# Normalising an attention group one step later in a software pipeline

## The chip, the cores and the metric

The kernel runs on one core of a Trainium2 chip. The metric is the device time of one execution in microseconds (us); lower is better. A core has TensorE (PE, matrix products and transposes), VectorE (DVE), ScalarE (ACT), GpSimd (POOL) and SyncE (SP, which issues the transfers here). Each engine works through its own list of instructions in order, and they wait for each other through semaphores.

## The reference

Sliding-window attention with a few sink tokens, then two gated layers:

```python
scores = scale * q @ k.T                      # 2 x 8 heads, 768 tokens, head size 64
keep = is_sink | in_window                    # 4 sinks, window of 128
a = exp(where(keep, scores, -1e9) - rowmax)
a = a / (sum(a) + 1e-9)
x = (a @ v)  -> [1536, 512]
x = (silu(x @ w_gate) * (x @ w_val)) @ w_out            # 512 -> 1536 -> 512
h = x @ w_in; out = (max(h,0) + alpha * min(h,0)) @ w_out2   # 512 -> 2048 -> 512
```

The inputs are normal random numbers; weights come as 64-bit floats and are split on the chip into a high and a low half for three matrix products in place of one.

## The kernel before

Attention is cut into 24 groups: one batch, one pair of heads, two blocks of 128 queries each (`NG` = 2). Eight groups of the first kind (query blocks 0 and 1) have no separate sinks and come first; from group 8 on a group has sink columns of its own. `attention` is a software pipeline of 27 steps. In step x it issues, in this order:

- `scores(x)`: four score products on PE (L217, tile `ps_s`); on DVE for each its masked row maximum (L223, for the later kind after a masked copy L221); on ACT its exponentials with row sums (L227, tiles `pr` and `ssum`);
- `values(x-3)`: the products of probabilities and values on PE (L313, L316, tile `xp`), then ACT's copy `xh` (L805) and DVE's remainder `xl` (L806);
- `flips(x-2)`: transposes of the normalised probabilities on PE (L272, and L295 for the sinks), copied out of PSUM into `pt`: groups 0 to 7 by ACT (L280) and DVE (L278), later ones by ACT (L283, L296) and then cut at the window by two selects on POOL (L284, L288);
- `norm(x)`: on DVE the row sums plus epsilon (L243) and their inverse (L244, tile `rinv`), and on POOL the products of `pr` with it (L250 for groups 0 to 7, L259 and the sinks' L260 for later ones). PE's flips of the group need these products.

Between these places the caller (`fast`) puts the work of the weight stream and of the first layer. One weight tile costs ACT a scaled copy (L520), DVE three bit operations (L536, L539, L542), ACT the high half (L550) and POOL the low half `wl` (L557). Such a conversion stands behind the flips in steps 2, 4, 6 and 7. From step 10 on the first layer's products (L613 to L615, L681 to L683) are mixed in, so PE has other work beside the attention; after the last group PE goes through the two layers alone.

DVE's list keeps the order in which the program is written (a manual schedule). The lists of PE, ACT, POOL and SP are set by a scheduler that works with its own model of times. PSUM has eight buffers (`ps`), shared by all: a product that finds none free waits for the reader of an old one. `pr` and `sk` have three buffers, `ssum` and `rinv` four, `pt` two.

Of the kernel before, what the change touches and what calls it, by code (L numbers as in the profile page):

```python
# [321 lines left out]
def attention(groups, begin):  # L322
    n = len(groups)

    def stage(f, x):
        if x < n:
            return getattr(groups[x], f)()

    stage("load", 0)
    begin[0]()  # L330
    stage("load_v", 0)
    stage("load", 1)
    stage("load", 2)
    begin[1]()
    for x in range(n + LAG + 1):
        if x < n:
            for t in range(NG):
                groups[x].scores(t)
        yield "before values", x, x - LAG - 1
        if x > LAG:  # L340
            groups[x - LAG - 1].values()
        yield "values", x, x - LAG - 1
        if LAG <= x < n + LAG:
            for t in range(NG):
                groups[x - LAG].flip(t)
        yield "flips", x, x - LAG - 1
        if x < n:
            groups[x].norm()
        stage("load", x + 3)
        stage("load_v", x + 1)  # L350
        if x == 14:
            begin[2]()
# [422 lines left out]
def fast(nc, tc, ctx, g, lim, alpha, qk, vp, vs, w_gate, w_val, w_out, x2_in, x2_out, out):  # L775
# [21 lines left out]
    with ExitStack() as inner:  # L797
# [26 lines left out]
        for at, x, last in attention(groups, (begin_a, begin_b, begin_c)):  # L824
            done = max(0, last + (at != "before values"))
            if at == "values" and done in (per, 2 * per):
                ready.append(m1.unit(0, done // per - 1))
            if done < per:
                if at == "flips" and st.n_conv < EARLY:
                    st.tick(1 + (done > 1))  # L830
            elif at == "before values" or at == "flips" and x in TWICE:
                product()
# [105 lines left out]
```

## Time and profile before

| | us |
|---|---|
| median of 3 runs | 683.36 (682.8 to 683.9) |
| the profiled execution, its own time | 680.56 |
| its span, first to last instruction | 678.8 |
| PE busy in the span | 657.4 (97%) |
| DVE busy | 391.7 (58%) |
| ACT busy | 297.8 (44%) |
| POOL busy | 79.9 (12%) |
| mean granted TensorE clock | 0.987 of full speed |

How to read it: every duration below is of this one profiled execution, whose own time is 680.56 us; 1.8 us of it lie outside the span. PE is close to full over the whole, but matmuls are pipelined, and the mean says little of the first stage, in which PE is free for about a fifth of the time. What any edit of the attention is worth has to be read there and in the mixed stage behind it.

### The profile page before, as it was taken

What the parts mean: (1) busy time and instruction counts of PE and PEld (TensorE: products, weight loads), DVE (VectorE), ACT (ScalarE), POOL (GpSimd) and SP (SyncE); (2) the same over time, 40 slices, a digit from 0 to 9 for tenths busy, and PEclk for the clock granted to TensorE, in tenths of its full rate; (3) what the DMA queues carried; (4) which work ended last, traced back from release to release, by engine and by line L of the source; (5) the groups of instructions that cost most, each with busy time, mean ns of one, the idle gap of its engine ahead of it and who ended that gap; (6) DMA issues with size and microseconds to landing.
All of it is one profiled execution on the core that took longest, in us unless ns stands there. A gap on an engine that the chain in (4) does not pass through costs nothing.

```text
span 678.8 us, 8589 instructions
## 1 busy us (share of the span) xinstructions
PE 657.4 (97%) x3098; PEld 519.5 (77%) x3098; DVE 391.7 (58%) x880; ACT 297.8 (44%) x680; POOL 79.9 (12%) x137
## 2 busy tenths in 40 slices
PE   7889889999999999999999999999999999999996
PEld 4555666767788888888888888888888888888885
DVE  5896858444289932389432789419834744334332
ACT  4778765656366612155221546336622333112320
POOL 3554644333100000000000000000000000000000
PEclk8989899999999999999999999999999999999998
DMA  9653535200045520045200034203400000000111
GB/s 264 180 169 115 166 114 168 69 24 24 1 155 186 169 79 1 0 125 181 68 0 1 33 124 129 89 1 93 156 1 0 1 0 1 1 0 8 55 63 67
DMA packets 37203, 52.29 MB, mean 77 GB/s; under 512 B 4384, under 2 KB 28960, under 8 KB 37152
## 3 DMA queue, kind: packets, MB, share of 16 engines
q1 hardware_dynamic: 34944, 51.65, 24.0%
q8 instruction: 26, 0.43, 0.2%
q10 hardware_dynamic: 2208, 0.01, 0.2%
q14 instruction: 25, 0.20, 0.1%
HBM read 48.51 MB, written 3.15 MB: 76 GB/s over the span
## 4 chain that ended last, share of the span: by engine, by line
PE 84%; DVE 7%; ACT 5%; issue 1%; POOL 1%; DMA 1%; SPq 0%; ACTq 0%; POOLq 0%
PE ph L615 6%; PE ph L613 6%; PE pf L739 6%; PE pf L737 6%; PE pf L738 6%; PE ph L614 6%; PE po L681 5%; PE po L682 5%; PE po L683 5%; PE pv L613 4%; PE pg L613 4%; PE pv L615 4%; PE pv L614 4%; PE pg L614 4%; PE pg L615 4%; PE xp L313 2%
## 5 line engine op out<-in xcount | busy, mean ns | idle before, releaser
L626 ACT ACTIVATE hh<-hid 128x512 fp32r<-128x512 f32 x84 | 53.1, 632 | 70.5 <-DVE hid L665 41.2
L627 DVE TENSOR_TENSOR hl<-hid,hh 128x512 fp32r<-128x512 f32 x84 | 57.9, 689 | 36.5 <-ACT hh L626 36.4
L613 PE MATMUL ph<-yh,wh 128*128 128x512 f32 x192 | 74.8, 390 | 0.0
L615 PE MATMUL ph<-yh,wl 128*128 128x512 f32 x192 | 74.7, 389 | 0.0
L737 PE MATMUL pf<-wh,hh 128*128 128x512 f32 x192 | 74.7, 389 | 0.0
L738 PE MATMUL pf<-wl,hh 128*128 128x512 f32 x192 | 74.7, 389 | 0.0
L614 PE MATMUL ph<-yl,wh 128*128 128x512 f32 x192 | 74.7, 389 | 0.0
L719 ACT ACTIVATE neg<-ph,sal 128x512 f32<-128x512 f32 x48 | 33.0, 687 | 93.4 <-PE ph L615 93.4
L739 PE MATMUL pf<-wh,hl 128*128 128x512 f32 x192 | 72.1, 389 | 0.0
L550 ACT ACTIVATE wh<-w_m 128x512 fp32r<-128x512 f32 x68 | 42.6, 630 | 55.8 <-DVE w_m L542 17.4
L721 DVE SCALAR_TENSOR_TENSOR hid<-ph,sig,neg 128x512 f32<-128x512 f32 x48 | 35.9, 749 | 38.4 <-ACT neg L719 38.0
L613 PE MATMUL pg<-xh,wh 128*128 128x512 f32 x144 | 57.6, 401 | 0.0
L613 PE MATMUL pv<-xh,wh 128*128 128x512 f32 x144 | 56.9, 395 | 0.3 <-ACT pt L283 0.3
L614 PE MATMUL pg<-xl,wh 128*128 128x512 f32 x144 | 57.0, 396 | 0.0
L615 PE MATMUL pg<-xh,wl 128*128 128x512 f32 x144 | 56.6, 393 | 0.0
L681 PE MATMUL po<-hh,wh 128*128 128x512 f32 x144 | 56.5, 394 | 0.0
L614 PE MATMUL pv<-xl,wh 128*128 128x512 f32 x144 | 56.2, 391 | 0.0
L682 PE MATMUL po<-hh,wl 128*128 128x512 f32 x144 | 56.2, 391 | 0.0
L615 PE MATMUL pv<-xh,wl 128*128 128x512 f32 x144 | 56.1, 390 | 0.0
L744 DVE TENSOR_TENSOR acc<-pf,acc 128x512 f32<-128x512 f32 x36 | 23.2, 686 | 52.0 <-PE pf L739 52.0
L683 PE MATMUL po<-hl,wh 128*128 128x512 f32 x144 | 53.2, 390 | 0.0
L557 DVE TENSOR_TENSOR wl<-w_m,wh 128x512 fp32r<-128x512 f32 x56 | 38.2, 686 | 21.6 <-ACT wh L550 21.5
(106 smaller groups left out, 1198.0 us busy)
## 6 DMA issues: line engine op xcount, KB each, us to landing
w_raw<-in_moe_w_out SPq DMA_DIRECT2D x28, 512.0 KB, 3.4
w_raw<-in_moe_w_in SPq DMA_DIRECT2D x16, 512.0 KB, 3.8
w_raw<-in_moe_w_gate SPq DMA_DIRECT2D x12, 512.0 KB, 3.7
w_raw<-in_moe_w_val SPq DMA_DIRECT2D x12, 512.0 KB, 3.6
th<-in_qk SPq DMA_DIRECT2D x16, 336.0 KB, 3.0
vr<-in_v SPq DMA_DIRECT2D x16, 192.0 KB, 2.4
out<-acc SPq DMA_DIRECT2D x12, 256.0 KB, 2.2
th<-in_qk SPq DMA_DIRECT2D x8, 256.0 KB, 5.5
```

Of the source, the lines that this page charges most:

```text
L550: nc.scalar.activation(wh, m, AF.Copy)
L613: nc.tensor.matmul(ps, wh[:, c], xh[:, kk], start=(kk == 0), stop=False)
L614: nc.tensor.matmul(ps, wh[:, c], xl[:, kk], start=False, stop=False)
L615: nc.tensor.matmul(ps, wl[:, c], xh[:, kk], start=False, stop=(kk == KD - 1))
L626: nc.scalar.activation(hh, hid, AF.Copy)
L627: nc.vector.tensor_tensor(out=hl, in0=hid, in1=hh, op=ALU.subtract)
L681: nc.tensor.matmul(ps, wh[:, mc], hh, start=(x == 0), stop=False)
L682: nc.tensor.matmul(ps, wl[:, mc], hh, start=False, stop=False)
L683: nc.tensor.matmul(ps, wh[:, mc], hl, start=False, stop=(x == CHUNK - 1))
L737: nc.tensor.matmul(ps, hh[:, ts], wh, start=(x == 0), stop=False)
L738: nc.tensor.matmul(ps, hh[:, ts], wl, start=False, stop=False)
L739: nc.tensor.matmul(ps, hl[:, ts], wh, start=False, stop=(x == CHUNK - 1))
```

## The change

`norm` is issued for group x-1 instead of group x, in the same place of step x, and so there is one more of its places at the end (step 24) and none in step 0:

```diff
         yield "flips", x, x - LAG - 1
-        if x < n:
-            groups[x].norm()
+        if 0 < x <= n:
+            groups[x - 1].norm()
         stage("load", x + 3)
```

The first place is DVE's list in step 3 (names end in a running number; `ps_s` is a score tile, `ssum` the row sums that the exponentials leave, `rinv` the inverse). Before, from the first maximum of group 3 on:

```order
L223 ISA ps_s_271,nb_111<-ps_s_271,mask_0_68 128x128
L223 ISA ps_s_272,nb_111<-ps_s_272,mask_0_68 128x128
L223 ISA ps_s_279,nb_111<-ps_s_279,mask_1_69 128x256
L223 ISA ps_s_280,nb_111<-ps_s_280,mask_1_69 128x256
L806 TENSOR_TENSOR xl_91<-xp_287,xh_90 128x256
L278 COPY pt_294<-ps_p_299 128x2x256
L243 TENSOR_SCALAR rinv_308<-ssum_269 128x4
L244 RECIPROCAL rinv_308<-rinv_308 128x4
```

After, the same stretch:

```order
L223 ISA ps_s_266,nb_111<-ps_s_266,mask_0_68 128x128
L223 ISA ps_s_267,nb_111<-ps_s_267,mask_0_68 128x128
L223 ISA ps_s_274,nb_111<-ps_s_274,mask_1_69 128x256
L223 ISA ps_s_275,nb_111<-ps_s_275,mask_1_69 128x256
L806 TENSOR_TENSOR xl_91<-xp_282,xh_90 128x256
L278 COPY pt_289<-ps_p_294 128x2x256
L243 TENSOR_SCALAR rinv_303<-ssum_218 128x4
L244 RECIPROCAL rinv_303<-rinv_303 128x4
```

The kinds of instruction stand in the same order; only the last two work on other data. Before, `ssum_269` belongs to group 3, whose maxima stand just above; after, `ssum_218` belongs to group 2, and the inverse of group 3 comes one step later.

The second place is POOL's list around steps 14 and 15 (`pt_1195` before and `pt_1189` after are the transposed probabilities of group 13, `pr_1010` and `pr_1004` the probabilities of group 14). Before:

```order
L288 AFFINE_SELECT pt_1070<-pt_1070 128x2x128
L259 TENSOR_TENSOR pr_1010<-pr_1010,rinv_1115 128x2x2x128
L260 TENSOR_TENSOR sk_1118<-pr_1010,rinv_1115 128x128
L557 TENSOR_TENSOR wl_1109<-w_m_1055,wh_1108 128x512
L284 AFFINE_SELECT pt_1195<-pt_1195 128x2x128
```

After:

```order
L557 TENSOR_TENSOR wl_1103<-w_m_1049,wh_1102 128x512
L284 AFFINE_SELECT pt_1189<-pt_1189 128x2x128 x2
L288 AFFINE_SELECT pt_1189<-pt_1189 128x2x128 x2
L259 TENSOR_TENSOR pr_1004<-pr_1004,rinv_1206 128x2x2x128
L260 TENSOR_TENSOR sk_1209<-pr_1004,rinv_1206 128x128
```

The normalising products of group 14 stood ahead of the selects of group 13 and now stand behind them.

The third place is PE's list in step 16, where group 13's values end and group 14 is transposed. Before:

```order
L316 MATMUL xp_1261<-pts_1208,vsr_113 128x128 x2
L272 MATMUL ps_p_1273<-ident_61,pr_1010 128x128 x2
L272 MATMUL ps_p_1279<-ident_61,pr_1010 128x128 x2
L681 MATMUL po_1246<-hh_944,wh_1177 128x512
L295 MATMUL ps_p2_1286<-ident_61,sk_1118 128x128
L681 MATMUL po_1289<-hh_679,wh_963 128x512
```

After:

```order
L316 MATMUL xp_1255<-pts_1202,vsr_113 128x128 x2
L681 MATMUL po_1240<-hh_938,wh_1171 128x512
L272 MATMUL ps_p_1267<-ident_61,pr_1004 128x128 x2
L272 MATMUL ps_p_1273<-ident_61,pr_1004 128x128 x2
L295 MATMUL ps_p2_1280<-ident_61,sk_1209 128x128
L681 MATMUL po_1283<-hh_673,wh_957 128x512
```

One product of the first layer (L681) has moved ahead of the transposes. PE's list up to step 13 is the same as before.

## Rows read from the trace of the kernel before

**Rows 1.** Stretches: length, busy us of PE, PEld, DVE, ACT, POOL, then PEclk, DMA.
```profile
0.00:48.50 48.50, 39.66 (x213) 23.92 (x214) 38.36 (x158) 30.55 (x116) 23.50 (x37) 0.89 0.69 204
48.50:110.00 61.50, 56.03 (x301) 38.44 (x299) 44.28 (x142) 43.49 (x121) 31.01 (x48) 0.97 0.46 145
110.00:180.00 70.00, 68.95 (x409) 49.88 (x406) 30.18 (x120) 38.90 (x113) 25.40 (x53) 1.00 0.15 45
180.00:678.80 498.80, 492.70 (x2183) 407.22 (x2181) 278.91 (x465) 184.86 (x331) 0.00 (x0) 1.00 0.19 61
```

**Rows 2.** Waits: who waited for whom, us in total, times, longest us.
```profile
DVE rinv L243 <- ACT pr L227: 4.1, 5, 1.7
```

**Rows 3.** Timeline, DVE, first inverse: start, duration, form, [idle before and releaser].
```profile
10.40 0.17 DVE L243 TENSOR_SCALAR rinv<-ssum 128x4 f32<-128x4 f32 x1 [1.67 <-ACT pr L227]
```

**Rows 4.** Timeline, PE, transposes of groups 0, 3, 5 and 8.
```profile
12.60 0.86 PE L272 MATMUL ps_p<-ident,pr 128*128 128x128 f32 x4 [0.52 <-POOL pr L250]
...
24.33 0.88 PE L272 MATMUL ps_p<-ident,pr 128*128 128x128 f32 x6
...
33.24 1.43 PE L272 MATMUL ps_p<-ident,pr 128*128 128x128 f32 x6
...
48.05 0.66 PE L272 MATMUL ps_p<-ident,pr 128*128 128x128 f32 x4
```

**Rows 5.** Timeline, DVE, steps 6 to 9: copies of flips, one bit operation, inverses.
```profile
31.65 0.68 DVE L278 COPY pt<-ps_p 128x512 f32<-128x512 f32 x1
32.25 0.42 DVE L536 TENSOR_SCALAR w_m<-w_m 128x512 int32<-128x512 int32 x1
...
34.04 0.16 DVE L243 TENSOR_SCALAR rinv<-ssum 128x4 f32<-128x4 f32 x1
...
35.87 0.68 DVE L278 COPY pt<-ps_p 128x512 f32<-128x512 f32 x1
36.47 1.24 DVE L536 TENSOR_SCALAR w_m<-w_m 128x512 int32<-128x512 int32 x1
...
42.11 0.68 DVE L278 COPY pt<-ps_p 128x512 f32<-128x512 f32 x1
...
45.74 0.68 DVE L278 COPY pt<-ps_p 128x512 f32<-128x512 f32 x1
```

**Rows 6.** Timeline, POOL, step 6: normalising products, then a weight's low half.
```profile
34.58 1.61 POOL L250 TENSOR_TENSOR pr<-pr,rinv 128x256 f32<-128x256 f32 x2 [4.05 <-DVE rinv L244]
36.15 1.27 POOL L557 TENSOR_TENSOR wl<-w_m,wh 128x512 fp32r<-128x512 f32 x1
```

**Rows 7.** Stretch of 2 us, columns as in Rows 1.
```profile
34.00:36.00 2.00, 2.00 (x10) 1.53 (x10) 1.97 (x13) 2.00 (x9) 1.42 (x2) 0.50 0.53 119
```

**Rows 8.** Timeline, POOL, normalising products of groups 12, 14 and 15.
```profile
75.08 1.04 POOL L259 TENSOR_TENSOR pr<-pr,rinv 128x512 f32<-128x512 f32 x1 [2.91 <-DVE rinv L244]
...
96.23 1.04 POOL L259 TENSOR_TENSOR pr<-pr,rinv 128x512 f32<-128x512 f32 x1 [3.91 <-DVE sig L98]
...
106.01 1.04 POOL L259 TENSOR_TENSOR pr<-pr,rinv 128x512 f32<-128x512 f32 x1 [4.90 <-ACT wh L550]
```

**Rows 9.** Timeline, PE, transposes of groups 11, 13 and 14.
```profile
76.34 0.60 PE L272 MATMUL ps_p<-ident,pr 128*128 128x128 f32 x4
...
96.52 0.60 PE L272 MATMUL ps_p<-ident,pr 128*128 128x128 f32 x4
98.82 0.33 PE L295 MATMUL ps_p<-ident,sk 128*128 128x128 f32 x1 [1.70 <-ACT pr L227]
...
104.76 0.38 PE L272 MATMUL ps_p<-ident,pr 128*128 128x128 f32 x2
105.60 0.44 PE L272 MATMUL ps_p<-ident,pr 128*128 128x128 f32 x2 [0.46 <-DVE xl L806]
```

**Rows 10.** Timeline, DVE, two later inverses: groups 13 and 15.
```profile
81.16 0.37 DVE L243 TENSOR_SCALAR rinv<-ssum 128x4 f32<-128x4 f32 x1 [1.04 <-ACT pr L227]
...
105.46 0.16 DVE L243 TENSOR_SCALAR rinv<-ssum 128x4 f32<-128x4 f32 x1
```

## The prediction

> **What bounds the kernel now.** I read the busy times by stretch first. From 180 us on (498.8 us) PE works on the two layers alone, at full clock, busy for 492.7 us; no attention is left there, and nothing in it changes. From 110 to 180 us PE is busy for 68.95 of 70 us. Only ahead of that does PE have time to spare: 8.8 us of the first 48.5, in which it has nothing but attention and DVE is the fuller engine beside it (38.4 busy), and 5.5 us of the next 61.5, the mixed stage [rows 1]. So the change can matter by what it does to the length of the first stage, and by stalls of PE in the mixed one; from there on a delay of PE goes to the end almost whole, since 1.05 us of idle time is all that could take it up before 180 us.
>
> Next the waits. DVE's sum (L243) waits for ACT's exponentials five times, 4.1 us in all [rows 2]; this is what the edit can take away. The first of them is the largest: at 10.40 us DVE has stood for 1.67 us while the scores of group 1 were already there [rows 3]. What the edit gives in exchange is distance: before, the normalising products of a group are issued two steps ahead of its transposes, after, one. So the other question for the trace is how long PE's transposes stand behind POOL's products, and I went through the first stage and the mixed one transposition by transposition.
>
> **The change part by part.** No instruction is added or removed, 24 pairs L243/L244 and POOL's products stay. The SP list has its loads in nearly the old order, and loads are not what these steps wait for; I cost that at nothing.
>
> *First stage, the gain.* DVE goes from the maxima of group 0 straight to those of group 1, 1.67 us plus the two instructions earlier, about 2.0. The inverse of group 0 is still taken at about 10.4, because ACT's sums come then, so its transposes are unchanged at 12.60 to 13.46 [rows 3, 4].
>
> *First stage, the price: a new loop.* From there step follows step by one chain: DVE copies the transposes of group x-2, then takes the inverse of group x-1, POOL multiplies, PE transposes that group, DVE copies it in the next step. Its links: copy to next DVE instruction 0.60 (31.65 to 32.25); start of L243 to start of POOL 0.54 (34.04 to 34.58); POOL 1.61 [rows 5, 6]; the last four of six transposes, 0.88 x 4/6 = 0.59 at full clock [rows 4]; two hand-overs, 0.15 together (POOL ends at 12.55, PE goes on at 12.60, and as much again to DVE, an estimate from that). Sum 3.5 us. In a step with a weight's bit operations 1.79 comes on top (32.25 to 34.04): 5.3 us.
>
> Now the copies one after the other. Group 0: 13.55 (transposes end at 13.46). Step 2 has bit operations: group 1 at 18.85; group 2 at 22.35; step 4: 27.65; 31.15; step 6: 36.45. Step 7 to step 8 DVE's own work is longer than the loop: before it takes 6.24 (35.87 to 42.11), of which 0.82 is L536 at 1.24 in place of 0.42, so 5.4: group 6 at 41.9; and 3.63 (42.11 to 45.74) for group 7: 45.5. Before, this last copy is at 45.74 [rows 5]. The inverse of group 8 follows at 46.1, POOL's 1.04 (length as in [rows 8]) ends at about 47.7, and group 8's transposes can start then; before they start at 48.05 [rows 4]. The early 2.0 us are used up by the loop, and by this sum the stage ends 0.35 early. My links are short estimates at two places, so I take 0. Bounds: -2.0 (the loop is hidden and the early gain stays) and +1.4 (0.2 more on each of the seven loops).
>
> One place where the Trainium skill bears on this. L536 took 1.24 us where it takes 0.42 otherwise, and ended 0.3 after POOL's L557 of 1.27, which had begun 0.32 us ahead of it [rows 5, 6]. The Trainium skill, page "SBUF — State Buffer", section "Who interferes with whom", says that VectorE in its two-port modes and GpSimd take their shared pair of ports in turn, each for a whole instruction; by that rule the trace agrees. By it the loop would lose up to about 1.1 us more (1.27 less 0.16) wherever a low half falls on the inverse, and the sum would be +3.1 with one such meeting; without one, as I have it, +2.0.
>
> *First stage, PE's clock.* The loop now holds PE's transposes, and PE stands before them for longer at a time (it waits for POOL with the scores and values done). In this trace PE's granted clock falls to half, 1.2 GHz, after such thinly filled times: it is 0.50 from 34 to 36 us, and six transposes take 1.43 instead of 0.88 [rows 4, 7]. Before, DVE and not PE bounds those steps, so it is hidden. In the loop one such stretch costs at least 0.37 (four of six transposes), and up to 1.5 if the scores behind them, also at half speed, push the next transposes back. One or two more or less costly stretches: +0.6, bounds 0 and +3.
>
> *Mixed stage.* PE has products of the first layer between the attention's, so most transposes find their probabilities ready: I compare each start on PE with the place on POOL where, after, that group's products will stand (those of the next group now). Group 11: POOL ends at 76.12, PE starts at 76.34, 0.2 to spare. Group 13: POOL would end at 97.27, PE starts at 96.52, late by 0.75; but PE stands until 98.82 for PSUM behind these transposes, so it costs nothing. Group 14: POOL begins at 106.01 and ends at 107.05, because DVE reaches that inverse at 105.46 only, behind two weight conversions; PE is there at 104.76 [rows 8 to 10]. After, both pairs run from 107.1 to 107.7 where before they end at 106.04, 1.66 later; less 0.23 for the one product now ahead of them (492.7 us for 2183 recorded matmuls [rows 1]): +1.4 us of PE. Bounds: 0 (DVE comes there earlier) and 107.1 - 104.76 = 2.3. For the other groups 0, bounds 0 and +1.4 (a second one like group 14).
>
> *Mixed stage, the gain.* The largest wait here, 1.04 at 81.16 [rows 10], lets, once gone, the maxima of group 14 begin 1 us earlier, but ACT, which has to follow, is itself held by its list. I take 0, bound -2.4 (all 4.1 but the first 1.67).
>
> Sum: 0 + 0.6 + 1.4 + 0 = +2.0 us on the profiled execution's 680.56, 682.6. That execution lies 2.8 below the median of the runs; the same +2.0 on 683.36 gives 685.4.
>
> **The rivals.**
>
> *Level.* PE's stall at group 14 is taken up later (group 13's 0.75 already costs nothing, and 1.05 us of idle time lies at 110 to 180), and the clock does no worse than before: 683.4, within 0.6. For it: the first stage comes out level link by link, and a stall of the in-order PE hits only one group of 24. Against: DVE's place for that inverse is set by its list, and nothing in the change moves it forward.
>
> *Faster.* The removed waits are worth more than the distance: the 2.0 us of the first step stay, because the loop is shorter than I add up (its hand-overs, or POOL's first product letting the first transposes go). Its price is decided in steps 2 to 5: if the copy of group 3 comes 2 us ahead of its 27.65, the gain stays. Time 683.36 - 2.0 = 681.4. For it: 4.1 us of waits do go, and no work is added. Against: the loop, whose links are each a row.
>
> *The clock falls more often.* PE waits longest in the steps with bit operations, of which the loop has four; two or three of them end in a stretch at half clock, each with 1 to 1.5 us on the loop: +3 in the first stage, and 1.4: 683.36 + 4.4 = 687.8. For it: the mean clock is 0.89 in the thinly filled first stage and 1.00 from 110 us on, where PE is full [rows 1]. Against: it falls after some thin times only, and PE's work per step is the same as before. The Trainium skill, page "TensorE: Matmul & The Clock Gate", section "What's actually happening", says that the low clock is the default and that activity releases it; the rows agree in their direction, and by that rule this case would be the likelier one.
>
> **How the numbers follow.** A difference below 0.2% (1.4 us) can't be told from no change here. The forecast, slower by about 2 (from 0.8 to 3.3): 0.50. Level: 0.26. Faster: 0.11. The clock: 0.13. Of the forecast's share about a fifth lies under 1.4 us: slower 0.50 x 0.8 + 0.13 + 0.02 (from the top of level) = 0.55; the same 0.10 + 0.24 = 0.34; faster 0.11. Likeliest: 685.4, its own range 684.1 to 686.7. The range reaches down to 682.3 (half of the faster case left out) and up to 688.2 (the clock case in).
>
> **What would show it.** Right: no wait of L243 for the exponentials; the maxima of group 1 at about 8.7 us (10.40 less 1.67); in steps 3 to 7 PE's transposes and DVE's copies waiting for POOL's L250; the transposes of group 8 at 48 to 49 us; those of group 14 waiting for POOL until DVE has passed two weight conversions, 1 to 2 us. Wrong: group 8's transposes earlier than 47 or later than 50 us, or group 14's without a wait; or a different length after 180 us, where I count no change.

## The result, and the profile after

| | before | after |
|---|---|---|
| median of 6 runs each, us | 682.87 (680.47 to 683.9) | 686.83 (685.26 to 688.09) |
| the profiled execution, own time | 680.56 | 688.09 |
| its span | 678.8 | 686.3 |
| mean granted TensorE clock | 0.987 | 0.979 |

The ratio of the runs is 1.0066 [1.0042, 1.0089]: slower by 4.5 us (2.9 to 6.1) on 682.87 us, where +2.0 was forecast. The two medians are 4.0 us apart. (Below, a ratio is turned into us in the same way.) Executions far off the rest of their kernel (704.5 and 2704.5 us of the changed kernel with zero products, 823.3 us of the mixed half, 1649.5 us of the kernel before) are in none of the ratios; the profiled execution of after is the slowest of its six, and that of before lies within 0.1 us of its fastest. Between these two the difference is 7.5 us, and what the two traces show has to be read with that in mind.

The stretches of after, columns as in [rows 1] (length, busy us of PE, PEld, DVE, ACT, POOL, then PEclk and DMA):

```profile
0.00:48.50 48.50, 37.67 (x195) 21.18 (x197) 33.95 (x142) 28.91 (x109) 20.70 (x33) 0.79 0.66 196
48.50:110.00 61.50, 53.41 (x295) 36.47 (x293) 44.38 (x137) 41.77 (x115) 28.83 (x43) 0.97 0.43 132
110.00:180.00 70.00, 68.30 (x387) 49.02 (x388) 34.14 (x136) 39.47 (x121) 28.28 (x55) 0.98 0.21 62
180.00:686.30 506.30, 500.05 (x2225) 412.79 (x2223) 279.38 (x466) 187.14 (x337) 2.42 (x7) 1.00 0.19 60
```

In the first 48.5 us every engine gets less done than in [rows 1], and the granted clock is 0.79 instead of 0.89. From 180 us on the program is only shifted.

The waits of after, up to 190 us (who waited for whom, us in total, times, longest), with the sum's own wait from the view of DVE as the last row:

```profile
PE ps_p L272 <- POOL pr L250: 7.8, 10, 1.9
DVE pt L278 <- PE ps_p L272: 6.4, 6, 1.7
PE ps_p L272 <- POOL pr L259: 2.5, 3, 1.3
...
DVE rinv L243 <- ACT pr L227: 0.4, 1, 0.4
```

The 4.1 us of [rows 2] have become 0.4. In their place PE's transposes wait for POOL's products and DVE's copies for the transposes: the loop that the prediction described. DVE's list around the first inverse (start, duration, form, idle before and releaser), answering to [rows 3]:

```profile
8.60 0.32 DVE L223 CUSTOM_DVE_ANT_0 ps_s<-ps_s,mask 128x128 f32<-128x128 f32 x1
...
10.38 0.17 DVE L243 TENSOR_SCALAR rinv<-ssum 128x4 f32<-128x4 f32 x1 [0.39 <-ACT pr L227]
```

The maxima of group 1 begin at 8.60 (8.7 was forecast), the inverse is taken at the old time. PE's transposes of groups 3 to 8 (the first row of each), as in [rows 4]:

```profile
26.19 0.60 PE L272 MATMUL ps_p<-ident,pr 128*128 128x128 f32 x2 [1.94 <-POOL pr L250]
...
31.30 1.54 PE L272 MATMUL ps_p<-ident,pr 128*128 128x128 f32 x6
...
36.48 0.64 PE L272 MATMUL ps_p<-ident,pr 128*128 128x128 f32 x2 [1.81 <-POOL pr L250]
...
42.24 0.69 PE L272 MATMUL ps_p<-ident,pr 128*128 128x128 f32 x2
...
47.43 0.88 PE L272 MATMUL ps_p<-ident,pr 128*128 128x128 f32 x6
...
51.67 0.66 PE L272 MATMUL ps_p<-ident,pr 128*128 128x128 f32 x4 [0.58 <-POOL pr L259]
```

Group 8 starts 3.6 us later than in [rows 4]; 48 to 49 us was forecast, and "later than 50" was named as the sign of an error. The clock of the stretches between (columns as above, PEclk third from the end):

```profile
26.00:28.00 2.00, 1.41 (x6) 0.93 (x6) 0.89 (x5) 1.78 (x9) 2.00 (x3) 0.58 0.85 244
28.00:30.00 2.00, 2.00 (x12) 1.12 (x12) 1.52 (x8) 1.16 (x5) 0.87 (x2) 0.50 0.14 48
...
34.00:36.00 2.00, 0.67 (x8) 0.29 (x4) 1.93 (x7) 1.00 (x3) 0.18 (x1) 1.00 0.51 136
...
40.00:42.00 2.00, 2.00 (x12) 0.77 (x8) 1.90 (x8) 0.63 (x1) 0.43 (x1) 0.50 0.07 13
...
44.00:46.00 2.00, 2.00 (x10) 1.19 (x8) 1.42 (x6) 1.20 (x6) 0.88 (x2) 0.50 0.61 218
```

In both places PE has just waited (1.94 and 1.81 us), and then its clock goes to half (1.2 GHz): from about 26 to 33 us and again from about 37 to 47. Before, the like of it are two shorter spells, of about 3 us each, around 34 to 36 [rows 7] and 44 to 46. The change also moved some of ScalarE's copies in this stage; whether that costs anything is answered below, by a run that has them nearly in the same places.

PE in the mixed stage, groups 13 and 14, answering to [rows 9], and a stretch behind:

```profile
101.43 0.66 PE L272 MATMUL ps_p<-ident,pr 128*128 128x128 f32 x4 [1.33 <-POOL pr L259]
103.32 0.30 PE L295 MATMUL ps_p<-ident,sk 128*128 128x128 f32 x1 [1.23 <-ACT pr L227]
...
110.06 0.49 PE L681 MATMUL po<-hh,wh 128*128 128x512 f32 x1 [1.06 <-ACT wh L550]
...
111.15 0.66 PE L272 MATMUL ps_p<-ident,pr 128*128 128x128 f32 x4 [0.59 <-POOL pr L259]
```
```profile
112.00:114.00 2.00, 2.00 (x6) 1.59 (x6) 1.33 (x7) 1.85 (x9) 2.00 (x5) 0.50 0.78 263
```

Group 13's L295 stands 4.5 us later than in [rows 9], group 14's L295 (111.64, before 106.26) 5.4, and group 15's first transpose (123.29, before 115.60) 7.7; from there to the end the shift stays at 7.5 to 7.7. So in this execution the first stage lost 3.6 us and the mixed stage 4.1. Of the latter, 2.3 us are lost between groups 14 and 15, with the clock at half from 112 to 115 us, where it was at 1.00 before; 0.9 up to group 13, most of it between groups 11 and 12, where both kernels have a spell at half clock of the same length; and 0.9 between groups 13 and 14.

### The profile page after: what moved, and what is told of

Read it like the earlier page. It is cut to its first block, busy times and chain, and to the rows that moved or that the text cites. A ratio compares the mean times of both kernels' runs of the same rounds, so it can differ in the third digit from the quotient of the medians.

```text
span 686.3 us, 8590 instructions
## 1 busy us (share of the span) xinstructions
PE 659.4 (96%) x3098; PEld 519.5 (76%) x3098; DVE 391.9 (57%) x880; ACT 297.3 (43%) x680; POOL 80.2 (12%) x137
## 4 chain that ended last, share of the span: by engine, by line
PE 85%; DVE 4%; ACT 4%; POOL 3%; issue 1%; DMA 1%; SPq 0%; POOLq 0%; ACTq 0%
PE ph L613 6%; PE ph L615 6%; PE pf L739 6%; PE pf L737 6%; PE pf L738 6%; PE ph L614 6%; PE po L681 5%; PE po L682 5%; PE po L683 5%; PE pv L613 4%; PE pg L613 4%; PE pv L614 4%; PE pv L615 4%; PE pg L614 4%; PE pg L615 4%; PE ps_s L217 2%
## 5 line engine op out<-in xcount | busy, mean ns | idle before, releaser
L681 PE MATMUL po<-hh,wh 128*128 128x512 f32 x144 | 57.4, 401 | 1.1 <-ACT wh L550 1.1
```

What stands on the lines that cost most here:

```text
L681: nc.tensor.matmul(ps, wh[:, mc], hh, start=(x == 0), stop=False)
```

## The experiments

Each kernel ran beside the kernel before on the same chip. What they have in common first: where PE's granted clock was below 1.00 from 20 to 50 us in the profiled execution, when group 8's transposes started in it, and the time of all runs against before.

| kernel | clock below 1.00 | group 8, us | against before, us |
|---|---|---|---|
| before | 32 to 38, 42 to 48 | 48.05 | |
| after | 26 to 34, 36 to 48 | 51.67 | +4.5 |
| first stage only | 26 to 34, 36 to 48 | 51.36 | +3.9 |
| after, group 14 in its old step | 26 to 32, 36 to 42 | 49.70 | +4.5 |
| before with zero products | none | 47.97 | -0.1 |
| first stage only with zero products | none | 47.70 | -1.8 |
| normalised ahead of the values | 36 to 48 | 47.89 | -3.7 |
| the same with zero products | none | 47.82 | -3.3 |

### Which half of the change costs it

Groups 0 to 7 alone one step later:

```diff
-        if x < n:
-            groups[x].norm()
+        for y in ([x - 1] if 0 < x < 9 else [8, 9] if x == 9 else [x] if 9 < x < n else []):
+            groups[y].norm()
```

> The inverse comes one step later for groups 0 to 7 only (the first stage); in step 9 groups 8 and 9 are both done, and from there on each group in its own step as before. Theory A (the loop copy, inverse, POOL, transposes carries the first stage, and PE's clock falls in it): group 8's transposes start 2 to 4 us later than before, none waits for POOL in the mixed stage; total +1.5 to +3.5 us, ratio 1.002 to 1.005. Rival B (the cost lies in the mixed stage, at group 14 alone): +0 +- 0.7.

Measured: 1.0057 [1.0038, 1.0076], +3.9 us (2.6 to 5.2). Almost the whole loss lies here, at or above the upper end of what Theory A had put there; group 8's transposes, 3.3 us later than before, are where it had them. Within this one program the time goes roughly with the clock of the execution: two with a mean of 0.968 took 688.9 us, three with 0.985 took 683.9 to 684.2, though the profiled one, at 0.979, took 684.2 too. The mean doesn't say where the half clock fell: the kernel before, at 0.985, took 680.6 to 682.0.

Groups from 10 on alone (`[x] if x < 10 else [x - 1] if 10 < x <= n else []`):

> The inverse comes in its own step up to group 9 as before, and one step later from group 10 on. Theory A: the first stage keeps its length (group 8's transposes at 48 us); group 14's transposes wait for POOL or a weight, 1 to 2 us, and with a fall of the clock behind it 2 to 4 us: +1 to +4 us, ratio 1.0015 to 1.006. If only the first stage matters: +0 +- 0.7.

Measured: 1.0019 [1.0005, 1.0033], +1.3 us (0.3 to 2.3). The size is that of the prediction's term; its cause is taken up below. The two halves add up to 5.2, within the interval of the whole; that the mixed half costs anything on top of the first can't be told from the runs (1.0066 against 1.0057).

### Is it the loop, or the clock in the loop

Eight products of zeros go into the PSUM tile of the transposes, ahead of them, in the places where PE waits (`g.zero` is a tile that the kernel has; the transposes overwrite the result):

```diff
         ps = g.ps_t.tile([P, 512], F32, tag="ps", name="ps_p")
+        if t == 0 and self.fill:
+            for _ in range(self.fill):
+                nc.tensor.matmul(ps, g.zero[:, 0:P], g.zero, start=True, stop=True)
...
+            groups[x - LAG].fill = 8 if x - LAG in (1, 3, 5, 6) else 0
             for t in range(NG):
                 groups[x - LAG].flip(t)
```

> The changed kernel with added work: eight products of zeros (128x512 out, about 0.2 us each at full clock) on TensorE ahead of the transposes of groups 1, 3, 5 and 6, where it stands longest for POOL. Their result is overwritten by the transposes. Theory A (the half clock lengthens the loop of copy, inverse, POOL's product and transposes): the granted clock stays at 1.00 over most of 26 to 48 us, six transposes take 0.9 us instead of 1.1 to 1.5, and group 8's transposes start at 48.5 to 50.3 us instead of 51.7; the time is +1.5 to +3 us above the kernel before instead of +4. Rival B (the loop's own links are longer than summed, the clock only follows): the clock may rise, but group 8's transposes stay at 51 to 53 us and the time at +4 to +6.

Measured: 1.0015 [1.0000, 1.0030], +1.0 us (0 to 2.0): some 3.5 of the 4.5 us are gone, though PE has work added. (By the medians it is +1.7 against +4.0, so 2.3 are gone.) Its profiled execution, the one of 704.5 us, had a granted clock of 0.85 from 20 to 80 us and never half clock there, and group 8 comes 3 us earlier than the 51.67 of after, where Theory A had it:

```profile
48.69 0.71 PE L275 MATMUL ps_p<-ident,pr 128*128 128x128 f32 x4 [0.23 <-POOL pr L259]
```

> The kernel before with the same added products of zeros in the same four places, as a control. Theory A: here VectorE and not TensorE bounds these steps, so the clock's two falls at 34 to 36 and 44 to 46 us go and group 8's transposes stay at 47.5 to 48.5 us; the time is within -0.5 to +1 us. Rival B, the same as A here. Rival C (a fill helps by itself, wherever a clock falls): -1 to -3 us, and group 8's transposes before 47 us.

Measured: 0.9999 [0.9983, 1.0014], -0.1 us. The clock is full from 20 to 62 us here too, and group 8's transposes start at 47.97 us instead of 48.05. What helps the changed kernel is worth nothing in the kernel before: there PE's half clock lies beside other work. Rival C falls.

> The first-stage-only change (groups 0 to 7 normalised one step later, all others in their old step) with the same added products of zeros ahead of the transposes of groups 1, 3, 5 and 6. Theory A (of the first stage's +3.9 us the half clock is 3 or more): clock 1.00 from 20 to 48 us, steps without bit operations 3.3 to 3.7 us and steps with them 5.2 to 5.6, group 8's transposes at 48.0 to 49.2 us, time within -0.5 to +1.2 us of the kernel before. Rival B (the loop costs it at full clock too): group 8's transposes at 50 us or later, time +2.5 to +4.5.

Measured: 0.9974 [0.9961, 0.9988], -1.8 us, and group 8 at 47.70: both better than Theory A's ranges, and far from Rival B's. Its transposes of groups 3 to 8 (the first row of each: start, duration, form, idle before; the line numbers are 3 higher than before), and its clock:

```profile
25.91 0.44 PE L275 MATMUL ps_p<-ident,pr 128*128 128x128 f32 x2
...
29.42 0.44 PE L275 MATMUL ps_p<-ident,pr 128*128 128x128 f32 x2 [0.16 <-POOL pr L250]
...
34.72 0.44 PE L275 MATMUL ps_p<-ident,pr 128*128 128x128 f32 x2
...
40.02 0.44 PE L275 MATMUL ps_p<-ident,pr 128*128 128x128 f32 x2
...
43.65 0.44 PE L275 MATMUL ps_p<-ident,pr 128*128 128x128 f32 x2
...
47.70 0.66 PE L275 MATMUL ps_p<-ident,pr 128*128 128x128 f32 x4 [0.43 <-POOL pr L259]
```
```profile
28.00:30.00 2.00, 1.70 (x14) 0.79 (x12) 1.81 (x11) 1.88 (x8) 1.33 (x3) 1.00 0.49 128
...
40.00:42.00 2.00, 1.44 (x11) 0.97 (x12) 1.91 (x10) 1.77 (x9) 2.00 (x2) 1.00 0.86 281
```

A step without bit operations takes 3.51 us (25.91 to 29.42), one with them 5.30 (29.42 to 34.72): the prediction's 3.5 and 5.3. Group 8 starts 0.35 us earlier than before, which is the prediction's sum for a loop at full clock. (That it agrees to the hundredth is luck: the sum was of links rounded to about 0.1.) So the loop is there and costs nothing at full clock; the first half without the zero products, at half clock in two spells, has group 8 at 51.36, 3.66 later:

```profile
51.36 0.66 PE L272 MATMUL ps_p<-ident,pr 128*128 128x128 f32 x4 [0.58 <-POOL pr L259]
```

The lists of VectorE and GpSimd are the same in these two kernels through the first stage, and PE's but for the zero products; ScalarE's differs in a few places, where a copy has changed places with its neighbours. (The -1.8 us of the whole is not the first stage's alone: between groups 8 and 10 another 2.45 us are won, along with another order on ScalarE, as in the run on the first wait below.)

The changed kernel with group 14 in its old step has the same lists in the first stage on every engine, ScalarE's too, and by chance its second spell at half clock ended early. Its transposes of groups 6 and 7, and the clock:

```profile
40.98 0.44 PE L272 MATMUL ps_p<-ident,pr 128*128 128x128 f32 x2
...
44.61 0.44 PE L272 MATMUL ps_p<-ident,pr 128*128 128x128 f32 x2
```
```profile
42.00:44.00 2.00, 2.00 (x15) 1.28 (x16) 1.90 (x9) 1.90 (x9) 1.21 (x2) 1.00 0.91 320
```

The step takes 3.63 us; in after, with the clock at 0.50 from 38 to 46 us, it takes 5.19 (42.24 to 47.43). The same instructions in the same order, 1.56 us apart by the clock; group 8 comes at 49.70 instead of 51.67. So the clock is shown as the cause of that part also without the zero products.

### The bit operations ahead of the transposes

```diff
-                if at == "flips" and st.n_conv < EARLY:
+                if at == "values" and st.n_conv < EARLY:
```

> The changed kernel, with the weight conversions of steps 2, 4, 6 and 7 issued ahead of the transposes rather than behind them, so that VectorE's three bit operations (1.8 us a tile) stand ahead of the copy and outside the loop of copy, inverse, POOL's product and transposes. Theory A (the loop carries the first stage): each of these four steps is shorter by 0.8 to 1.8 us, group 8's transposes start at 45 to 48.5 us instead of 51.7, and the time is -2.5 to +1 us against the kernel before. Rival E (VectorE's whole load carries it, in whatever order): group 8's transposes at 50.5 to 52 us, time +3 to +4.5.

Measured: 1.0118 [1.0095, 1.0141], +8.0 us, a clear miss. DVE in step 4 (as above):

```profile
21.21 0.42 DVE L806 TENSOR_TENSOR xl<-xp,xh 128x256 fp32r<-128x256 f32 x1 [0.59 <-ACT xh L805]
21.55 0.42 DVE L536 TENSOR_SCALAR w_m<-w_m 128x512 int32<-128x512 int32 x1
...
23.34 0.68 DVE L278 COPY pt<-ps_p 128x512 f32<-128x512 f32 x1
```

The operations stand ahead of the copy, but behind `xl`, which waits for the values of the same step. The transposes end at 21.76; the copy comes at 23.34, 1.6 later, for DVE is still busy. Nothing has left the loop, so the run doesn't do what it was made for and can't speak for Theory A or against it. Group 8 comes at 50.99, where Rival E had it, but the time fits neither; the other 5 us of the loss come behind it, where ScalarE's list and the clock differ again. Rival E falls by the zero products: with the same load on VectorE group 8 came at 47.70.

### The removed waits by themselves

Only the first inverse moves, the one with the 1.67 us [rows 3] (`[0, 1] if x == 1 else [x] if 1 < x < n else []`):

> As before, but the inverse of group 0 stands behind the maxima of group 1, directly ahead of the inverse of group 1. It takes away the one wait of 1.67 us at the start and makes no loop. Theory A: the maxima of group 1 come 2 us earlier, the inverse of group 1 still waits for ACT and comes 0.5 us earlier: -0.6 to 0. Rival C (that wait is worth its 2 us): -2.

Measured: 0.9962 [0.9949, 0.9974], -2.6 us (-3.5 to -1.8): the size of Rival C, and outside Theory A. But group 8's transposes come at 48.35, no earlier than in [rows 4]: in the first stage the wait was worth nothing, so Rival C's reason is wrong as well. The gain stands in steps 10 to 12, in ScalarE's list, which the scheduler had set otherwise:

```profile
55.73 1.28 ACT L657 ACT_TABLE_LOAD   x1
57.03 0.60 ACT L657 ACTIVATE sg<-pg 128x512 f32<-128x512 f32 x1
...
58.18 0.58 ACT L657 ACTIVATE sg<-pg 128x512 f32<-128x512 f32 x1
...
61.57 1.28 ACT L227 ACT_TABLE_LOAD   x1
```

Two gate functions (`sg`) stand together between the exponentials; in the kernel before, each has a table load of 1.28 us on either side (loads at 54.40, 56.31, 59.13 and 63.83). One pair of loads fewer, 14 instead of 16 in the whole program, and group 10's transposes come at 63.95 instead of 66.20. This gain comes with a list that the edit doesn't name: the scheduler set it. The first half with zero products has the same 14 loads and nearly the same gain (2.45 us between groups 8 and 10). That the order on ScalarE is the cause is read from the traces; no run changes it alone.

The distance restored without the wait: norm(x-1) right behind the maxima of group x, ahead of values, transposes and bit operations:

```diff
             for t in range(NG):
                 groups[x].scores(t)
+        if 0 < x <= n:
+            groups[x - 1].norm()
         yield "before values", x, x - LAG - 1
```

> The inverse of group x-1 is taken in step x as in the changed kernel, but directly behind the maxima of group x, ahead of values, of the copy of the transposes and of the weight's bit operations. No wait for the exponentials, and the copy is no longer a link between two inverses, so the loop is open. Theory A: neither the first stage's loop nor group 14's stall is left; group 8's transposes at 45 to 48 us; 0 to -3 us against before, 4 to 7 below the changed kernel. Rival D (any inverse one step later costs, whatever its place): +2 to +4 as the changed kernel.

Measured: 0.9946 [0.9927, 0.9965], -3.7 us; this beats both kernels. Group 8 comes at 47.89, only 0.16 earlier than before; most of the gain is again behind it (group 10 at 62.99, 3.2 earlier), where two gate functions stand together again, though the whole program has 16 loads.

> The version that normalises a group right behind the next group's maxima, ahead of the values (-3.7 us against the kernel before), with the same added products of zeros in the four places. Theory A (its first stage loses most at half clock from 36 to 48 us, where eight score products take 3.4 us instead of 1.7): those stretches go and group 8's transposes start at 45.5 to 47 us instead of 47.9; time -4.5 to -6 us against the kernel before. Rival G (its first stage is bound by ScalarE and VectorE, and its gain lies in ScalarE's list in the steps behind it): group 8's transposes stay at 47.5 to 48.5, time -3 to -4, or less if the fill delays.

Measured: 0.9952 [0.9939, 0.9965], -3.3 us, no gain over the version without. Its clock is full from 18 to 78 us and group 8 still comes at 47.82. Rival G holds: with the normalisation out of the way, PE is not what the first stage waits for.

### The mixed stage: group 14, or group 13

> The changed kernel, but group 14 alone is normalised in its old step (step 14 takes groups 13 and 14, step 15 none). Theory A (group 14's transposes wait for POOL, and the half clock from 112 to 116 us follows from that wait): that wait and that stretch at half clock go, group 14's transposes start 3.5 to 5 us later than in the kernel before instead of 6, and group 15's the same; the time is +1.5 to +3 us above the kernel before instead of +4. Rival D (what is lost there only shifts, since the first layer's products wait for weights anyway): +3.5 to +4.5, and the half clock is found near 112 us all the same.

Measured: 1.0066 [1.0044, 1.0088], +4.5 us, the same as the whole change. Theory A falls: group 14's wait for POOL is gone, and the time is not. The half clock has moved: it stands from about 102 to 109 us, behind a wait of 1.62 us of group 13's transposes for POOL.

> The mixed-stage-only change (groups from 10 on normalised one step later; alone it took +1.3 us), with group 14 back in its old step. Theory A, the prediction's term (group 14's late normalisation is what the mixed stage costs): the time is within -0.5 to +0.6 us of the kernel before, and group 14's transposes start at 104.5 to 106 us. Rival F (the other groups' distance, or a moved weight conversion, costs it): +0.9 to +2, group 14's transposes at 106.5 us or later. Rival D (the list changes it makes cost more than they save, as with group 14 alone in the changed kernel): over +2.

Measured: 1.0025 [1.0014, 1.0036], +1.7 us: no better than the mixed half with group 14 in it, and group 14's transposes start at 106.68 us, as Rival F had it. So group 14 is not what it costs. In this trace and in that of the mixed half, group 13's transposes wait for POOL (1.61 and 1.60 us). PE in the mixed half, and a stretch behind:

```profile
96.43 0.66 PE L272 MATMUL ps_p<-ident,pr 128*128 128x128 f32 x4 [1.60 <-POOL pr L259]
98.32 0.30 PE L295 MATMUL ps_p<-ident,sk 128*128 128x128 f32 x1 [1.23 <-ACT pr L227]
98.55 2.51 PE L217 MATMUL ps_s<-th 64*128 64x288 f32 x8
```
```profile
100.00:102.00 2.00, 2.00 (x7) 1.06 (x4) 1.69 (x5) 1.18 (x5) 0.00 (x0) 0.50 0.00 0
```

Before, the same eight score products took 1.61 us at full clock, behind one wait of 1.70 [rows 9]. Here PE has waited 1.60 and then 1.23, the clock goes to half, and they take 2.51. The last run moves group 13 alone back (PE's list stays as it is):

```diff
-        for y in ([x] if x < 10 else [x - 1] if 10 < x <= n else []):
+        for y in ([x] if x < 10 else [12, 13] if x == 13 else [x - 1] if 10 < x <= n and x != 14 else []):
```

> The mixed-stage-only change (+1.3 us alone) with group 13 back in its old step; TensorE's list is as in the mixed-stage-only change, to the row. Theory H (group 13's wait of 1.6 us for POOL brings TensorE's clock down behind it, 98 to 104 us, and that is the mixed stage's cost): the wait goes or falls below 0.5 us, the stretch 98 to 104 us is at 1.00 or half as long, group 14's transposes start at 104.5 to 106 us, and the time is within -0.6 to +0.6 us of the kernel before. Rival F (the distance of the other groups or the shift of a weight conversion costs it, and the clock falls there anyway behind the wait for the exponentials): +0.9 to +2, group 14's transposes at 106.5 us or later.

Measured: 0.9979 [0.9967, 0.9990], -1.4 us.

```profile
98.27 0.60 PE L272 MATMUL ps_p<-ident,pr 128*128 128x128 f32 x4
98.86 0.33 PE L295 MATMUL ps_p<-ident,sk 128*128 128x128 f32 x1
100.14 1.51 PE L217 MATMUL ps_s<-th 64*128 64x288 f32 x8 [0.96 <-ACT pr L227]
```
```profile
100.00:102.00 2.00, 1.86 (x10) 1.39 (x11) 1.93 (x6) 2.00 (x9) 1.56 (x3) 1.00 0.21 69
```

Both waits at group 13's transposes are gone, the eight score products behind them take 1.51 us after a wait of 0.96, and the clock stays at 1.00 from 98 to 106 us, while group 14 still waits for POOL (0.58 us at 107.14). The kernel is 2.7 us faster than the mixed half, more than Theory H gave it, and its time is below before; group 14's transposes, at 107.14, are where Rival F had them, in a profiled execution that is the slowest of its twelve (682.37 us, with spells at half clock at 62 to 68 and 80 to 88 us). That group 13's place decides is shown: the intervals of the two kernels don't meet. How it does is not shown, and the waits with the clock behind them, as Theory H has it, are not enough for it. In after, group 13's transposes have the same two waits (1.33 and 1.23 us, in the lines of the result), and the clock stays at 1.00 from 88 to 110 us. With the first inverse alone moved, the clock is at half from about 99 to 102 us behind a single wait of 1.72, much like the 1.70 that cost no clock in [rows 9]. And executions with the same mean clock, 0.987, took 681.8 and 682.1 us in the mixed half, but 679.9 and 680.1 here. The lists of DVE, POOL and ScalarE all change with the edit.

## Why the prediction was right or wrong

**Right.** The direction, and the mechanism of the loop: its links, 3.5 and 5.3 us a step, and the end of the first stage 0.35 early, measured as they were summed once PE's clock is kept up (5.3 in place of 5.4 in step 7). The early start of the maxima of group 1 (8.60), the unchanged first transposes (12.59 for the last four), and the waits of transposes and copies for L250 are all there. The gain of 2.0 was rightly taken as used up: the wait alone, moved, gives nothing in the first stage.

**The step that failed** is "First stage, PE's clock", with its "+0.6, bounds 0 and +3". In the traces it measures +3.66 us (group 8's transposes at 51.36 in the first half, 47.70 in the same with zero products; after's own 51.67 would make it 3.97), above the upper bound; over all runs the zero products take off 3.5 us (2.3 by the medians). I had the cause and priced it as one or two stretches of some 2 us, as in [rows 7], with 0.37 to 1.5 each. In the loop they last about 7 and 10 us: two steps without bit operations take 5.11 (26.19 to 31.30) and 5.19 (42.24 to 47.43) instead of 3.51 and 3.63, so 1.6 each, and the rest is spread over the steps beside them. The rival "the clock falls more often" (+3 in the first stage) was the nearest, with 0.13 of the chance: its sum of +4.4 is nearly the measured +4.5, and by the traces it was still low for the first stage. So the time of 686.83 lies in the range because the range took that case in; the likeliest value, 685.4, with its own range to 686.7, was too low. My own argument for 0.6, that "it falls after some thin times only, and PE's work per step is the same as before", overlooked that the wait becomes longer: 1.8 to 1.9 us in a row in steps 5 and 7 where before PE's longest wait for L250 was 0.6.

The Trainium skill, page "TensorE: Matmul & The Clock Gate", section "What's actually happening", has the low clock as the default, released by activity. The runs agree: products of zeros in the waits are enough to hold 1.00 from 18 to 76 us (the first half with them). The prediction said that by that rule this case would be the likelier one, and gave it the smaller chance all the same.

The other place: in the first stage of after no inverse meets a low half of a weight (all L243 there take 0.16 to 0.17 us), so the 1.1 us a meeting stayed out, as in the sum. Where they do meet, in the version normalised ahead of the values, one costs 0.73 us, within that bound; POOL and DVE there:

```profile
33.32 1.27 POOL L557 TENSOR_TENSOR wl<-w_m,wh 128x512 fp32r<-128x512 f32 x1 [2.47 <-ACT wh L550]
```
```profile
33.72 0.89 DVE L243 TENSOR_SCALAR rinv<-ssum 128x4 f32<-128x4 f32 x1
```

The sum takes 0.89 us in place of 0.16 and ends with POOL's product (34.61 and 34.59). The Trainium skill, "SBUF — State Buffer", "Who interferes with whom", says that VectorE in its two-port modes and GpSimd take their shared pair of ports in turn; this row agrees.

**The mixed stage: +1.4, from group 14.** The half alone measures +1.3, but not by group 14, so that the size agrees is luck. Group 14 does wait as I said (0.59 for POOL, and 1.06 in the product moved ahead of it), yet putting it back saves nothing. Group 13's lateness, of which the prediction says that "PE stands until 98.82 for PSUM behind these transposes, so it costs nothing", is what costs: with group 13 alone back in its old step 2.7 us are gone. Put at 0.75 us, that wait is 1.60 in the mixed half; the L295 behind it starts at 98.32 there, so the next instruction is indeed not late. I had counted a wait by whether the next instruction on PE is delayed, and nothing else. By which way that lateness costs stays open: the half clock behind it in the mixed half (about 99 to 102 us) can be a part of it, but after has the same waits without it.

**No change after 180 us** holds: the shift is 7.7 us at group 15 and 7.5 at the end. What stays open is how the two halves go together: in the profiled execution of after the mixed stage lost 4 us, in the medians no more than about 1 beyond the first stage's.

## What to carry to other kernels

Shortening the distance between a producer and the in-order engine that needs it can cost more than the wait itself when that engine is TensorE and the steps hang on a chain through it: price the wait, and then the half clock behind it on that chain. It need not cost: the version normalised ahead of the values has the same distance in steps, makes no such chain, and is the fastest here. A wait that "is covered" by a later one can cost all the same, and is worth a run of its own. And a small edit under a scheduler can win or lose more through a list that it reorders elsewhere than through what it does: compare the lists of all engines before giving a gain to the edit.

## What the hardware showed that I had not expected

- Spells at half clock in the first stage last about 7 and 10 us here, against about 3 in the kernel before. PE is busy through most of them (2.00 of 2.00 us in three of the stretches shown), so full work at half clock didn't end them at once. The loop alone doesn't explain their length: the version normalised ahead of the values has no such loop and is at half clock from 37 to 47 us too. Nor does the length of the wait before tell whether the clock falls: it fell at 26 us behind a wait of 1.05 us with the bit operations ahead, and not behind 1.33 and 1.23 at group 13 in after. What sets both is not shown.
- Idle time on PE that is filled with products of zeros is not lost time: 32 of them in four steps turned +4.5 us into +1.0, and cost nothing measurable in the kernel before (-0.1).
- One switch between exponentials and the gate function costs 1.28 us on ScalarE for the load, and the next instruction starts 1.29 to 1.30 us after the load did (54.40 to 55.69 before, 55.73 to 57.03 in the lines on the first wait). The Trainium skill, "ScalarE: Activation LUTs", section "What ACT_TABLE_LOAD costs", gives about 2.66 us for it with a drain; the load agrees, and of a drain these rows show nothing.
- Taking away 2.5 of the 2.8 us that DVE's sum waits within the first 49 us moved the end of the stage by 0.16 us (normalised ahead of the values) and 0.35 us (the first half with zero products). In the second of them DVE's copies wait 5.1 us for PE's transposes in the same stretch instead.
